# One split load, one moved load, half a value part ahead of five transposes and one dummy pair fewer, in the prologue of a mixed attention and FFN kernel

## Chip, core and metric

The kernel runs on one core of a Trainium2 chip (trn2). The metric is device time in microseconds (us): the median of several executions of the whole kernel. Lower is better. Engines are named as in the profile: PE (matrix engine; PEld is its weight load), DVE (vector), ACT (scalar activations), POOL, and SP, which only issues DMAs. ACT issues some DMAs too; its issues and SP's go into two different DMA queues.

## What is computed

For 2048 tokens of width 640 the result is `g * a + (1 - g) * b`, with a gate per token, a linear attention with 32 heads of width 20, and a SwiGLU FFN of width 1728:

```python
g = sigmoid((x * gate_w).sum(-1, keepdims=True))
# a: q, k, v = split(x @ wqkv); per head
pq, pk = q @ w_phi, k @ w_phi
phi = lambda p: concat(softmax(p), softmax(-p))
kv, z = phi(pk).T @ v, phi(pk).sum(tokens)
a = (phi(pq) @ kv / (phi(pq) @ z + 1e-6)) @ wo
# b
b = (silu(x @ w_gate) * (x @ w_up)) @ w_down
```

Everything is bf16 in memory.

## The kernel before

The 2048 tokens are 16 tiles of 128 (t = 0 to 15); the width of 640 is 5 chunks of 128 (c = 0 to 4). PE contracts over a chunk at a time, so x must stand transposed in `xT[:, t, c, :]`, and a product with 640 output columns is two groups of 320 columns in the two banks of a PSUM pair. There are four such pairs; `next_pair` gives the least recently used one that is not held.

The order of work is written out by hand in two strings. `LOADS` (line 33) gives the order in which the loads are issued; `ORDER` (line 38) gives the order in which every other piece is put into the engines' streams. Each token of the strings is a letter for a helper and its arguments. A tracker (`run`, line 145) adds the semaphore waits that the data needs. So each engine runs its own instructions strictly in the order of the strings, and waits where data or a buffer is not ready.

The pieces that matter here all lie in the first eight microseconds:

- `H` (`warm`, line 511): one dummy pair, that is two 128x128 matmuls on a constant tile. Their result is not used. There are 13 pairs at the head of `ORDER`.
- `X` (`xpose`, line 495): the transposes of token tile t = 0 to 3 by PE, five of them (line 338), and the copies from PSUM into `xT`. For t < 3 the first chunk goes into one bank and is copied by DVE, and the other four go into the second bank. For t = 0 (`X0.0`, `X0.1`) these four are copied by ACT, for t = 1 and 2 by DVE. The token tiles from t = 4 on are transposed by DMAs.
- `G` (`gcol`, line 505): one matmul of 5 columns and a DVE copy which puts the gate's weights beside the value weights, as column 640 of `wvg`.
- `U t.c` (`vpart`, line 539): a value part, the two matmuls (320 and 321 columns; the 321st is the gate's) of token tile t and chunk c of the value projection. Part c = 0 takes a pair and holds it; part c = 4 gives it back and lets ACT copy the result. The parts of the token tiles 0 to 2 are interleaved so that each chunk of weights is used three times soon after it has landed.
- `h` (`load_phi`, line 417) issues two small loads on ACT's queue, after ACT has waited for the landing of the value rows of chunk 3 (`wv_evs[3]`).

The first loads, in the order of `LOADS`, are spread over two queues by the lists `XQ` and `WQ` (lines 391 and 392). SP issues x0 (token tile 0, 160 KB), the gate's weights `gwr`, then the value rows `w1`, `w2`, `w3` (each 128 rows of `A_wqkv` with 640 columns, 160 KB), then the first columns of `wg` and `wu` (`f0`, 480 KB each), and then transposing DMAs (the key weights into `wT`, x4 and so on into `xT`). ACT issues `w0`, x1, x2, x3 and `w4`, and after them loads its function table.

Of the kernel before, what the change touches and what calls it, by code (L numbers as in the profile page):

```python
# [6 lines left out]
P = 128  # L7
S_TOK = 2048
D = 640
# [26 lines left out]
"""  # L36

ORDER = """
H0 H1 H2 H3 H4 H5 H6 H7 H8 H9 H10 H11 H12 X0.0 X0.1 G X1 h U0.0 U1.0 U0.1 X2 U1.1 U2.0 U0.2 U1.2
U2.1 X3 U2.2 U0.3 U1.3 U2.3 U0.4 U1.4 U2.4 V3 Y i4 F0.1 M0 M1 F0.2 M2 V4 M3 M4 F0.0 M5 K0 i3 K1 S0 I  # L40
P0 K3 S1 P1 F1.0 K2 V6 E0 V8 K4 S2 S3 E1 S4 K5 S5 P2 P3 V7 E2 V5 R0 K6 P4 P5 R2 E3 K7 S6 E4 V15 K8
E5 V10 S7 P6 K9 E6 R1 P7 S8 K10 S9 E7 K11 S10 V9 V11 P8 E8 K12 P9 R3 E9 P10 K13 S11 E10 K14 S12 P11
# [11 lines left out]
class _Tracker:  # L54
# [90 lines left out]
    def run(self, eng, fn, reads=(), writes=(), dma=False):  # L145
        rkeys = list(dict.fromkeys(k for a in reads for k in self.keys_of(a)))
        wkeys = list(dict.fromkeys(k for a in writes for k in self.keys_of(a)))
        need = {}

        def req(ev, raw):  # L150
            if ev is None:
                return
            s, v = ev
            if s == eng and not dma and (eng == "pe" or not raw):
                return
            if v > need.get(s, 0):
                need[s] = v

        for k in rkeys:
            for kk in self._conflicts(k):  # L160
                req(self.lastw[kk], True)
                if k[0] == "psum":
                    for s, v in self.readers[kk].items():
                        req((s, v), False)
        for k in wkeys:
            for kk in self._conflicts(k):
                req(self.lastw[kk], True)
                for s, v in self.readers[kk].items():
                    req((s, v), False)
        self._wait(eng, need)  # L170
        ins = fn()
        if dma:
            sn = "d%d" % self.ndma
            self.ndma += 1
            self._add_sem(sn)
            inc = 16
        else:
            sn, inc = eng, 1
        ins.then_inc(self.sem[sn], inc)
        self.cnt[sn] += inc  # L180
        v = self.cnt[sn]
        snap = dict(self.known[eng])
        if not dma:
            snap[sn] = max(snap.get(sn, 0), v)
        self.evknow.setdefault(sn, {})[v] = snap
        ev = (sn, v)
        for k in wkeys:
            self.lastw[k] = ev
            self.readers[k] = {}
        for k in rkeys:  # L190
            r = self.readers[k]
            if r.get(sn, 0) < v:
                r[sn] = v
        return ev


def _build(nc, A_x, A_wqkv, A_w_phi, A_wo, B_x, B_w_gate, B_w_up, B_w_down, gate_w, out):
    tr = _Tracker(nc)
    pe, act, dve, pool, sp = nc.tensor, nc.scalar, nc.vector, nc.gpsimd, nc.sync
# [3 lines left out]
    def sb(name, shape, dtype):  # L203
        t = nc.alloc_sbuf_tensor(name, list(shape), dtype)
        tr.reg(t, "sbuf", nc.lookup_mloc(t).addr)
        return t
# [3 lines left out]
    wvg = sb("wvg", [P, 5, D + 8], BF16)  # L210
# [95 lines left out]
    def bank(b, c0, c1, r0=0, r1=P):  # L306
        return ps[r0:r1, b * 512 + c0:b * 512 + c1]
# [9 lines left out]
    def mm(pairs):  # L317
        reads, writes = [], []
        for p in pairs:
            reads += [p[1], p[2]]  # L320
            writes.append(p[0])

        def fn():
            last = None
            for o, l, r, st, sp_, sk in pairs:
                last = pe.matmul(o, lhsT=l, rhs=r, start=st, stop=sp_, skip_group_check=sk)  # L326
            return last
        return run("pe", fn, list({id(a): a for a in reads}.values()), writes)
# [45 lines left out]
    def dma(e, dst, src, transpose=False):  # L374
        eo = tr.eng[e]

        def fn():
            if transpose:
                return eo.dma_start_transpose(dst, src)
            return eo.dma_start(dst, src)  # L380
        rd = [src] if src.tensor.name in tr.base else []
        wr = [dst] if dst.tensor.name in tr.base else []
        return run(e, fn, rd, wr, dma=True)
# [5 lines left out]


    XQ = ["sp", "act", "act", "act"]
    WQ = ["act", "sp", "sp", "sp", "act"]
    x2 = A_x[0]
    out2 = out[0]

    def load_rows(e, dst, c, c0):
        return dma(e, dst, A_wqkv[c * P:(c + 1) * P, c0:c0 + D])
# [11 lines left out]
    wv_evs = []  # L409

    def load_wv(c):
        wv_evs.append(load_rows(WQ[c], wvg[:, c, 0:D], c, 2 * D))

    def load_gate():
        dma("sp", gwr[0:5, :], bass.AP(gate_w.tensor, gate_w.offset, [[P, 5], [1, P]]))
# [68 lines left out]
    def used(r):  # L484
        ring["lru"].remove(r)
        ring["lru"].append(r)
        return r

    def next_pair():
        return used([r for r in ring["lru"] if r < ring["n"] and r not in held][0])  # L490
# [31 lines left out]
    def v_pairs(t, pr):  # L522
        return [(bank(2 * pr + hb, 0, 320 + hb), xT[:, t, c, :], wvg[:, c, 320 * hb:640 + hb - 320 * (1 - hb)],
                 c == 0, c == 4, False) for c in range(5) for hb in range(2)]

    def v_out(t, pr):
        i = halves(pr).rearrange("p b (h d) -> p b h d", d=DH)
        o = vbuf(t)[:, 0:H * (DH + 1)].rearrange("p (b h d) -> p b h d", b=2, d=DH + 1)[:, :, :, 0:DH]
        copy("act", o, i)
        copy("act", svec[:, t:t + 1], bank(2 * pr + 1, 320, 321))  # L530
# [5 lines left out]

    vpr = {}

    def vpart(t, c):

        if c == 0:
            vpr[t] = next_pair()
            held.add(vpr[t])
        mm(v_pairs(t, vpr[t])[2 * c:2 * c + 2])
        if c == 4:
            held.remove(used(vpr[t]))
            v_out(t, vpr[t])
# [398 lines left out]
    def kv_end():  # L946
# [4 lines left out]

    ops = {
        "H": lambda i: warm(), "i": fills, "X": xpose, "G": gcol, "U": vpart, "V": vtile,
        "M": lambda m: premult(1, m), "R": lambda m: premult(0, m),
        "K": ktile, "S": knorm, "P": kmul, "p": lambda t: kmul(t, "dve"), "E": kvtile, "x": load_x, "t": load_xt, "w": load_wv, "g": load_gate, "h": load_phi, "k": lambda m: load_wt(1, m), "q": lambda m: load_wt(0, m),
        "f": lambda i: load_ffn(FCUT[i], FCUT[i + 1]), "L": load_late_weights, "T": tail_weights, "J": gates,
        "Y": w_blocks, "I": kv_begin, "N": kv_end, "Z": z_row,
# [9 lines left out]
def bass_gated_mix__linear_kernel_hedgehog__swiglu_ffn__prompt_kernel(  # L967
    nc: bass.Bass,
    A_x: bass.AP,
    A_wqkv: bass.AP,  # L970
    A_w_phi: bass.AP,
    A_wo: bass.AP,
    B_x: bass.AP,
    B_w_gate: bass.AP,
    B_w_up: bass.AP,
    B_w_down: bass.AP,
    gate_w: bass.AP,
    out: bass.AP,
):
    _build(nc, A_x, A_wqkv, A_w_phi, A_wo, B_x, B_w_gate, B_w_up, B_w_down, gate_w, out)  # L980
# [28 lines left out]
```

## Time and profile before

| | |
|---|---|
| median of 3 runs | 285.66 us (285.46 to 285.72) |
| the profiled execution | 285.23 us, of which its span from the first to the last instruction is 284.0 us |
| PE busy | 280.9 us, 99% of the span |
| DVE, POOL, ACT busy | 190.5, 156.0, 139.6 us |
| DMA, first 12 us | 2.96 MB, 246 GB/s in the mean |

How to read it: the profile is one execution. A line of the timeline gives the start and the length in us, the engine (a `q` behind its name means its sequencer, here the issue of a DMA), the line of the kernel, the operation, the tiles as out<-in, the shape and how many instructions were merged; in brackets stands how long the engine was idle before it and what ended the idle time. The length of a merged PE line runs to the end of the last matmul, which includes its way through the array, so successive PE lines overlap. The chain of waits goes back from the last instruction to what released it, step by step. The landing of a DMA is the moment at which its semaphore is complete; the trace records each semaphore update.

### The profile page before, as it was taken

Reading aid. Unit: us, or ns where it says so; the run is one execution under the profiler, and the core shown is the slowest. Engines: PE = TensorE matmul, PEld = TensorE weight load, DVE = VectorE, ACT = ScalarE, POOL = GpSimd, SP = SyncE. Lnnn points to the kernel's source line nnn. Section 1 sums busy time; section 2 is a strip of 40 time slices with the busy share of each in tenths; the row PEclk is TensorE's granted clock in tenths of the full one; section 3 lists DMA queues with packets and bytes.
Section 4 is the critical chain, followed back from the end, with each engine's and each line's share of the span. In section 5 each row is a group of like instructions: output and inputs, shape, how many; then the busy total and the mean of one; then the engine's idle time right before and its main releaser. Section 6 shows DMA issues by size and latency. Waiting matters only on the chain.

```text
span 284.0 us, 4689 instructions
## 1 busy us (share of the span) xinstructions
PE 280.9 (99%) x1802; PEld 156.3 (55%) x1809; DVE 190.5 (67%) x280; ACT 139.6 (49%) x241; POOL 156.0 (55%) x119
## 2 busy tenths in 40 slices
PE   8999999999999999999999999999999999999997
PEld 7656777766645455445545445454544444444766
DVE  2336767684798888879999899997878355053100
ACT  2567777785755666657747764130101675001022
POOL 6277979987178858597868744463062553100100
PEclk9999999999999999999999999999999999999999
DMA  7976879100085252022340200623647510133411
GB/s 236 231 115 118 122 169 374 36 3 0 3 264 155 64 107 51 9 54 51 60 52 2 52 4 14 134 57 66 122 133 139 101 37 7 42 80 71 122 46 46
DMA packets 62085, 25.19 MB, mean 89 GB/s; under 512 B 51023, under 2 KB 61543, under 8 KB 62063
## 3 DMA queue, kind: packets, MB, share of 16 engines
q1 hardware_dynamic: 60534, 24.03, 37.4%
q10 hardware_dynamic: 1529, 0.87, 1.0%
q8 instruction: 14, 0.23, 0.4%
q14 instruction: 8, 0.07, 0.1%
HBM read 10.16 MB, written 2.63 MB: 45 GB/s over the span
## 4 chain that ended last, share of the span: by engine, by line
PE 99%; issue 0%; DVE 0%
PE ps L326 97%; PE ps L518 1%; PE ps L338 1%; DVE osb L934 0%
## 5 line engine op out<-in xcount | busy, mean ns | idle before, releaser
L354 POOL TENSOR_TENSOR hT<-hT,us 128x512 bf16<-128x512 bf16 (+1 forms) x37 | 43.6, 1185 | 43.4 <-DVE hT L358 33.6
L326 PE MATMUL ps<-xT,wg 128*128 128x512 bf16 x260 | 64.6, 379 | 0.0
L326 PE MATMUL ps<-xT,wu 128*128 128x512 bf16 x260 | 64.6, 379 | 0.0
L354 POOL TENSOR_TENSOR ph<-eq,qc 128x1320 bf16<-128x1320 bf16 x16 | 40.3, 2521 | 30.6 <-DVE qc L673 19.5
L326 PE MATMUL ps<-wqk,xT 128*128 128x320 bf16 x320 | 47.9, 299 | 0.0
L344 ACT ACTIVATE us<-ps 128x512 bf16<-128x512 f32 (+1 forms) x56 | 33.4, 597 | 22.0 <-PE ps L326 19.7
L326 PEld LDWEIGHTS ps<-xT,wu 128*128 128x128 bf16 x260 | 25.4, 98 | 30.7
L326 PEld LDWEIGHTS ps<-xT,wg 128*128 128x128 bf16 x260 | 24.9, 98 | 28.4 <-ACT oT L344 0.6
L354 POOL TENSOR_TENSOR ekr<-ekr,krec 128x1280 bf16<-128x1280 bf16 x16 | 37.3, 2357 | 5.8 <-DVE krec L368 5.8
L358 DVE SCALAR_TENSOR_TENSOR hT<-hT,ps 128x512 bf16<-128x512 bf16 (+1 forms) x37 | 25.0, 681 | 21.2 <-ACT hT L344 19.0
L344 ACT ACTIVATE eq<-ps 128x640 bf16<-128x640 f32 x32 | 22.3, 703 | 32.3 <-PE ps L326 31.2
L326 PEld LDWEIGHTS ps<-wqk,xT 128*128 128x128 bf16 x320 | 30.4, 98 | 13.3
L354 POOL TENSOR_TENSOR hx<-hx,us 128x512 bf16<-128x512 bf16 (+1 forms) x19 | 24.1, 1271 | 21.3 <-DVE hx L358 11.8
L344 ACT ACTIVATE hT<-ps 128x512 bf16<-128x512 f32 (+1 forms) x37 | 22.0, 596 | 25.0 <-PE ps L326 24.8
L365 DVE TENSOR_REDUCE ksum<-ekr 128x64 f32<-128x1280 bf16 x16 | 23.4, 1463 | 11.0 <-ACT ekr L344 11.0
L326 PE MATMUL ps<-hT,wd 128*128 128x512 bf16 (+1 forms) x137 | 30.6, 380 | 0.2
L344 ACT ACTIVATE ekr<-ps 128x640 bf16<-128x640 f32 x32 | 22.3, 703 | 6.9 <-PE ps L326 6.4
L326 PE MATMUL ps<-wvg,xT 128*128 128x320 bf16 (+1 forms) x160 | 24.1, 300 | 0.0
L365 DVE TENSOR_REDUCE qw<-ez 128x64 f32<-128x1280 bf16 x16 | 23.6, 1476 | 0.0
L365 DVE TENSOR_REDUCE qz<-eq 128x64 f32<-128x1280 bf16 x16 | 23.6, 1477 | 0.0
L354 DVE TENSOR_TENSOR ez<-eq,zb 128x1280 bf16<-128x1280 bf16 x16 | 21.9, 1385 | 0.3 <-DMA zb<-zrow 0.3
L326 PEld LDWEIGHTS ps<-hT,wd 128*128 128x128 bf16 (+1 forms) x140 | 13.0, 97 | 16.2 <-issue 1.3
(103 smaller groups left out, 288.5 us busy)
## 6 DMA issues: line engine op xcount, KB each, us to landing
wd<-in_B_w_down_dram SPq DMA_DIRECT2D x1, 2080.0 KB, 10.6
out_dram<-osb SPq DMA_DIRECT2D x2, 640.0 KB, 3.5
wg<-in_B_w_gate_dram SPq DMA_DIRECT2D x1, 1040.0 KB, 8.8
wu<-in_B_w_up_dram SPq DMA_DIRECT2D x1, 1040.0 KB, 9.9
wog<-in_A_wo_dram SPq DMA_DIRECT2D x2, 375.0 KB, 4.4
wg<-in_B_w_gate_dram SPq DMA_DIRECT2D x1, 640.0 KB, 5.2
wu<-in_B_w_up_dram SPq DMA_DIRECT2D x1, 640.0 KB, 6.4
omgb<-omgd SPq DMA_DIRECT2D x2, 256.0 KB, 4.0
```

Of the source, the lines that this page charges most:

```text
L326: last = pe.matmul(o, lhsT=l, rhs=r, start=st, stop=sp_, skip_group_check=sk)
L338: last = pe.transpose(o, i, ident[0:k, 0:k])
L344: return run("act", lambda: act.activation(o, i, func, scale=scale), rd, [o])
L354: return run(e, lambda: eo.tensor_tensor(o, a, b, op), [a, b], [o])
L358: return run("dve", lambda: dve.scalar_tensor_tensor(out=o, in0=a, scalar=s, in1=b, op0=op0, op1=op1), rd, [o])
L365: return run("dve", lambda: dve.tensor_reduce(o, i, AX.X, ALU.add), [i], [o])
L518: last = pe.matmul(bank(2 * pr, 0, P), lhsT=c, rhs=c, start=True, stop=True)
```

## The change

Four edits:

1. The value rows of chunk 0 are loaded by two DMAs of 320 columns (80 KB each) in place of one of 640 (160 KB), both on ACT's queue and still at its head. x1, x2 and x3 are issued behind both.
2. The value rows of chunk 4 are issued by SP, behind those of chunk 3 and ahead of `wg`, in place of ACT behind x3.
3. The value part U0.0 is cut into its two matmuls: `U0.0.0` (columns 0 to 319) stands behind `G` and ahead of x1's transposes, and `U0.0.1` (columns 320 to 640) stands where U0.0 stood. The first takes the pair.
4. There are 12 dummy pairs in place of 13.

The number of DMAs that ACT issues ahead of its function table stays five; SP issues one more. On PE's stream the only differences are two dummy matmuls fewer and one matmul of 320 columns five transposes earlier. The order of instructions on DVE, POOL and ACT (apart from its DMA issues) is the same.

```diff
 ORDER = """
-H0 H1 H2 H3 H4 H5 H6 H7 H8 H9 H10 H11 H12 X0.0 X0.1 G X1 h U0.0 U1.0 U0.1 X2 U1.1 U2.0 U0.2 U1.2
+H0 H1 H2 H3 H4 H5 H6 H7 H8 H9 H10 H11 X0.0 X0.1 G U0.0.0 X1 h U0.0.1 U1.0 U0.1 X2 U1.1 U2.0 U0.2 U1.2
...
     XQ = ["sp", "act", "act", "act"]
-    WQ = ["act", "sp", "sp", "sp", "act"]
+    WQ = ["act", "sp", "sp", "sp", "sp"]
...
     def load_wv(c):
-        wv_evs.append(load_rows(WQ[c], wvg[:, c, 0:D], c, 2 * D))
+        if c == 0:
+            dma(WQ[c], wvg[:, c, 0:320], A_wqkv[0:P, 2 * D:2 * D + 320])
+            wv_evs.append(dma(WQ[c], wvg[:, c, 320:D], A_wqkv[0:P, 2 * D + 320:3 * D]))
+        else:
+            wv_evs.append(load_rows(WQ[c], wvg[:, c, 0:D], c, 2 * D))
...
-    def vpart(t, c):
-
-        if c == 0:
+    def vpart(t, c, hb=None):
+
+        if c == 0 and not hb:
             vpr[t] = next_pair()
             held.add(vpr[t])
-        mm(v_pairs(t, vpr[t])[2 * c:2 * c + 2])
+        mm(v_pairs(t, vpr[t])[2 * c + (hb or 0):2 * c + (2 if hb is None else hb + 1)])
```

## The prediction

> **What bounds the kernel now.** I read the page's chain of waits first, then the chain in order of time, then the timeline of the first 30 us, then the trace's semaphore records for the exact landings. The page's chain:
>
> ```profile
> PE 99%; issue 0%; DVE 0%
> PE ps L326 97%; PE ps L518 1%; PE ps L338 1%; DVE osb L934 0%
> ```
>
> PE sets the end, and nothing else holds a share. From the chain in order of time:
>
> ```profile
> 0.84 2.93 PE ps L518 x26
> 3.78 0.02 issue
> 3.79 0.72 PE ps L338 x5
> ...
> 7.91 66.79 PE ps L326 x630
> ```
>
> I went through the starts of all matmuls for places where the next one comes later than the columns of the one before it allow. From 5.29 us on there is none worth naming (a 128-column matmul follows in 56 ns, a 320-column one in 136 ns; the jumps of 0.2 us far behind are matmuls missing from the records). So everything from U1.0's first matmul at 5.29 us on is a stream without a hole, and a change confined to the prologue can do only three things: move 5.29, tear a hole into the stream, or change PE's pace. The prologue:
>
> ```profile
> 0.81 0.41 ACTq L380 DMA_DIRECT2D wvg<-in_A_wqkv_dram  x1
> ...
> 0.84 2.93 PE L518 MATMUL ps<-const-bfloat16-1.0 128*128 128x128 bf16 x26 [0.84 <-PEq L994]
> ...
> 1.26 1.42 ACTq L380 DMA_DIRECT2D xs<-in_A_x_dram  x3
> ...
> 3.19 1.28 ACT L344 ACT_TABLE_LOAD   x1 [3.19 <-issue]
> ...
> 3.79 0.45 PEld L338 LDWEIGHTS ps<-ident,xs 128*128 128x128 bf16 x5 [0.28 <-DMA xs<-in_A_x_dram]
> ...
> 4.12 0.23 DVE L350 COPY xT<-ps 128x128 bf16<-128x128 bf16 x1 [4.12 <-PE ps L338]
> ...
> 4.41 0.70 PE L338 MATMUL ps<-ident,xs 128*128 128x128 bf16 x5
> 4.55 0.60 ACT L344 ACTIVATE xT<-ps 128x512 bf16<-128x512 bf16 x1
> ...
> 4.91 1.08 PE L326 MATMUL ps<-wvg,xT 128*128 128x320 bf16 x6
> ...
> 5.26 0.40 PEld L326 LDWEIGHTS ps<-wvg,xT 128*128 128x128 bf16 x4 [0.21 <-issue]
> ...
> 5.83 0.44 PE L338 MATMUL ps<-ident,xs 128*128 128x128 bf16 x5
> ```
>
> The reader is to see three things. (a) x0's transposes start at 3.79 on x0's landing (3.75 in the semaphore records), not on the end of the dummies: the weight load sat idle 0.28 us for the DMA. The last dummy starts at 3.465 and the dummies follow each other in 0.107 us, so PE ran dry at 3.57. (b) The gap of 0.21 us before 5.26 stands as "issue", but the instruction waits for ACT's copy of x0's other four chunks (4.55 to 5.15), both because U0.1 reads them and because U1.0's PSUM pair is the one that this copy empties. That copy began behind x0's last transpose (done at 4.52) and behind ACT's table load, which ended at 3.19 + 1.28 = 4.47. (c) PE runs at half pace at first: five transposes take 0.70 at 4.41 and 0.44 at 5.83; the starts are 0.107 us apart, then 0.056. The trace's first record of the full granted clock begins at 4.96.
>
> **One dummy pair fewer.** It removes 2 x 0.107 = 0.21 us of PE time in front of x0's transposes. PE would be dry at 3.36 in place of 3.57, and x0 lands at 3.75. Worth nothing: a wait of 0.22 becomes one of 0.43. It would be worth up to 0.21 only if x0 landed by 3.36.
>
> **The half part ahead of x1's transposes.** x0's first chunk is copied by DVE at 4.12 to 4.35, its semaphore comes at 4.36, and a matmul that waits for such a copy starts some 0.06 later (U2.0: semaphore 6.32, matmul 6.38). So U0.0.0 starts at about 4.42, just where x1's first transpose stood (4.41), and 320 columns at the half pace cost 2.5 x 0.107 = 0.27: x1's transposes start at 4.68. Three of them at 0.107 and two at 0.056 end at 5.11; U0.0.1 takes 0.14, and PE is at U1.0 by 5.25. Two waits hold U1.0 there. ACT's copy is unchanged, so its matmul is not before 5.29. And U1.0 reads x1's first chunk: from the first transpose of x1 to the semaphore of its copy were 4.97 - 4.41 = 0.56 us, so it now comes at 4.68 + 0.56 = 5.24, and U1.0 starts at about 5.31. **Sum: 5.31 - 5.29 = +0.02 us.** PE does the same work between 3.79 and 5.3 in another order, between the same two ends. Cover: x1's landing, which was 4.36, with PE asking for it at 4.40, may now come as late as 4.64. Behind U1.0 nothing is nearer: x1's second copy would end at about 5.8, and U1.1 reads it at 6.11.
>
> The most that can be won: if x0 landed earlier, ACT's copy still could not begin before 4.47 plus the 0.08 or less that it stood behind it. So 5.29 can go to about 5.21, and **-0.08 us is the floor** of the prologue as the change leaves it. PE can win no more by being early.
>
> **The split load.** ACT issues five DMAs ahead of its table before and after (0.81, three from 1.26 in 1.42, one at 2.70), so the table load stays at 3.19. x1, x2 and x3 are issued one step, about 0.48 us, later: 1.74, 2.22, 2.70. Their packets did not start at their issue but 2.0 to 2.5 us later (x1 issued 1.26, first packet 3.26; x2 1.74, 3.87; x3 2.22, 4.74), each within 0.05 us of the end of the block before it on the queue. The DMA engines are full from about 3 us on. So the later issue is hidden by the backlog, and what counts is what the split costs there. Rows of 640 bytes are not in the trace; the packet records give 36 ns for 768 bytes and 55 ns for 1280, so about 31 for 640 on the same line. A block of 160 KB is 8 rows on each of 16 engines: 8 x (2 x 31 - 55) = 0.06 us. From the other side, if a DMA of 128 rows costs a slot whatever its bytes, the split delays all that is behind it by one slot: the blocks start 0.4 to 0.5 us apart, say 0.45. Below nothing: x0 shares the engines with shorter packets, and may land up to 0.1 earlier, worth at most the 0.08 above. I take +0.06, as the row nearest in size gives it. The landings against PE's need (weight load) before:
>
> | | x1 | w1 | x2 | w2 | x3 | w3 | w4 |
> |---|---|---|---|---|---|---|---|
> | landed | 4.36 | 4.77 | 5.51 | 6.49 | 6.90 | 7.37 | 7.67 |
> | asked for | 4.40 | 5.42 | 5.70 | 6.53 | 7.34 | 7.89 | 8.70 |
>
> The thinnest margin is w2's, 0.04 us (one engine's update came 0.45 behind the other fifteen). With +0.06 PE waits 0.02 less the 0.02 by which it is itself late: nothing. With +0.45 it waits 0.4.
>
> [...]
>
> **The fifth rows on SP.** The bytes are the same and the engines are full until about 10 us, so the last of `wg` and `wu` lands as before (9.00 and 10.49; PE asks at 10.9 and 11.9). w4 itself now stands right behind w3 (7.37) and a block takes 0.45 us: 7.8 at the latest, or 8.3 with a slot's delay of w3, and 8.70 is asked. SP's issues behind it move by one issue, 0.43 us: `wg`, `wu`, and all transposes. The first of these is issued at 4.05 and takes 2.94 to issue, so it stood in a backlog that absorbs this. If it did not, the first key weights (landed 11.06, asked 12.96) have 1.9 us and the second (12.71, asked 13.39) 0.7. ACT's small loads wait for w3 (issue at 7.39 behind 7.37); w3 is no longer in competition with w4 and comes rather earlier. Their product is ready at 12.71 and PE loads it at 12.96: 0.25 us of cover. Cost: nothing.
>
> **The sum.** +0.02 (order) + 0 (dummies) + 0 (loads) on the profiled execution: 285.25. The profiled one is 0.43 below the median of 285.66; on the median that makes **285.7 us**, which is no change.
>
> **Rivals.**
>
> *PE's holes are closed.* PE is dry 0.22 us before 3.79 and 0.07 before 5.29. If in ordinary runs x0 lands earlier than here, or the shorter rows let it, both are won: -0.29, 285.4. For it: the profile is one execution, 0.43 from the median. Against it: ACT's table load, which holds U1.0 at 5.21 or later.
>
> *A DMA costs a slot.* The split puts 0.45 us on x1, x2, w2 and x3. PE waits at x1 (4.81 for 4.68), and in the end for w2, some 0.4 us in all, since each wait gives cover to the next: 286.1. For it: the issue takes 0.41 to 0.46 us whatever it moves, and the blocks' starts fit a slot as well as they fit the bytes. Against: the DMA share of 1.05 from 3 us on, which is full engines.
>
> *PE's clock comes later* (slower). The full clock came 4.1 us after the first dummy, with PE busy but for 0.22 us. With 0.43 us dry before x0's transposes the count could begin anew at 3.79, and the full clock come at 7.9 in place of 4.96. PE would run its stream from 4.96 to 7.9 at half pace and lose half of 2.9 us: +1.5, 287.2. It decides between an idle time of 0.22 us, which is shown to do no harm, and one of 0.43. For it: nothing in the rows but the removed pair. Against: the half part puts 0.27 us of matmul back before 4.96.
>
> [...]
>
> **Chances.** Forecast 0.62, holes closed 0.15, a slot 0.13, the clock 0.07, what I do not see 0.03. About 0.2%, 0.57 us, is what a measurement of this kernel can tell from no change: below 285.1 or above 286.2. The forecast, the holes and nearly all of the slot lie inside. Faster 0.04, slower 0.14 (the clock 0.07, a slot with a second wait 0.05, the rest), within 0.82. The range runs from the holes' 285.4 less the 0.2 by which the runs shown fall below their median, 285.2, to the slot's 286.1, and leaves out the clock.
>
> **What would show it.** Right: x0's transposes still start at x0's landing near 3.8 with an idle time of 0.4 before them; x1's transposes at 4.7; U1.0 at 5.3; x2's transposes at 5.8; no PE wait behind. Wrong: U1.0 before 5.2 or after 5.5; PE weight loads idle on `xs` or `wvg` between 5 and 8 us (a slot); x2's transposes 0.1 us apart (the clock).

## The result, and the profile after

The changed kernel takes 288.64 us (median of 4 runs, 288.12 to 288.90), the kernel before 285.56 us beside it. The ratio is 1.0088, 95% interval 1.006 to 1.0116: slower by 3.1 us (0.9%), clear of the noise, where 285.2 to 286.1 us were predicted. The profiled execution took 288.90 us with a span of 287.6; the one before took 285.23 with 284.0.

The page's chain of waits, after:

```profile
PE 97%; DMA 2%; ACTq 0%; DVE 0%; issue 0%
PE ps L326 96%; DMA xs<-in_A_x_dram 2%; ACTq L380 0%; PE ps L338 0%; DVE osb L938 0%
```

Before, PE alone stood there. Now a DMA into `xs`, one of x1 to x3, holds 2% of the span, and ACT's issue queue is in the chain. The chain in order of time (start, length, what) says where:

```profile
1.73 0.46 ACTq L380
2.18 0.03 issue
2.21 5.53 DMA xs<-in_A_x_dram
7.74 0.05 issue
7.78 0.45 PE ps L338 x5
8.24 2.64 PE ps L326 x10
10.88 0.53 PE ps L338 x5
11.41 66.92 PE ps L326 x630
```

It goes back from x2's transposes at 7.78 to x2's load, issued at 2.21, and to ACT's issues. From 11.41 on PE is again a stream of 66.92 us (66.79 before) and stays one to the end. So the loss lies ahead of 11.4 us. The timeline there, with the idle time of each engine in brackets:

```profile
3.18 1.28 ACT L344 ACT_TABLE_LOAD   x1 [3.18 <-issue]
...
3.49 0.45 PEld L338 LDWEIGHTS ps<-ident,xs 128*128 128x128 bf16 x5 [0.20 <-DMA xs<-in_A_x_dram]
3.50 0.71 PE L338 MATMUL ps<-ident,xs 128*128 128x128 bf16 x5
...
4.10 0.45 PE L326 MATMUL ps<-wvg,xT 128*128 128x320 bf16 x1
...
4.47 0.60 ACT L344 ACTIVATE xT<-ps 128x512 bf16<-128x512 bf16 x1
...
6.45 0.28 PEld L338 LDWEIGHTS ps<-ident,xs 128*128 128x128 bf16 x5 [2.25 <-DMA xs<-in_A_x_dram]
6.46 0.45 PE L338 MATMUL ps<-ident,xs 128*128 128x128 bf16 x5 [1.91 <-DMA xs<-in_A_x_dram]
...
6.75 0.98 PE L326 MATMUL ps<-wvg,xT 128*128 128x321 bf16 x5
...
7.78 0.28 PEld L338 LDWEIGHTS ps<-ident,xs 128*128 128x128 bf16 x5 [0.39 <-DMA xs<-in_A_x_dram]
7.78 0.45 PE L338 MATMUL ps<-ident,xs 128*128 128x128 bf16 x5
...
8.07 2.80 PE L326 MATMUL ps<-wvg,xT 128*128 128x320 bf16 x10
...
10.67 0.74 PE L338 MATMUL ps<-ident,xs 128*128 128x128 bf16 x5
...
11.21 3.61 PE L326 MATMUL ps<-wvg,xT 128*128 128x320 bf16 x24
```

Three things are to be seen. First, x0 came earlier than before: its transposes start at 3.50, not at 3.79, and the half part is done on time, at 4.10. Second, PE then stands still until 6.46, for x1, which landed at 6.41 by the semaphore records (4.36 before), and again at 7.78 for x2. x2's transposes stand 7.78 - 5.83 = 1.95 us later than before. Third, ten value matmuls take 2.80 us from 8.07 and five transposes 0.74 at 10.67, where the five at 7.78 took 0.45: PE is back at half pace. Busy time and granted clock of the four stretches of 3.41 us around this (columns: stretch, its length, busy time and number of instructions for each engine, granted clock, DMA share, GB/s):

```profile
core 0: us, PE busy (x) PEld busy (x) DVE busy (x) ACT busy (x) POOL busy (x), PEclk, DMA share, GB/s
1.32:4.73 3.41, 3.23 (x29) 2.63 (x26) 0.41 (x2) 1.54 (x2) 3.10 (x9) 1.00 0.69 185
4.73:8.14 3.41, 1.63 (x16) 1.01 (x17) 0.74 (x3) 0.34 (x1) 0.96 (x3) 1.00 1.00 310
8.14:11.55 3.41, 3.41 (x19) 2.10 (x17) 0.66 (x3) 0.00 (x0) 0.00 (x0) 0.50 1.22 265
11.55:14.97 3.42, 3.42 (x26) 2.41 (x25) 1.44 (x4) 2.02 (x7) 1.73 (x4) 1.00 1.12 177
```

The clock's column is full by default where the trace has no record, as for the first stretch, where the dummies stand 0.107 us apart, as x3's transposes do in the stretch recorded at 0.50 (x2's at 7.78: 0.056). The records are: full at 4.73 for 3.413 us, half from 8.143 for 3.413, full from 11.556 on. In the stretch from 4.73 to 8.14 PE was busy 1.63 of 3.41 us, and in the one behind it the clock was 0.50. PE never ran dry there, so half of 3.41, 1.71 us, was lost. Waits and clock together are 1.95 + 1.71 = 3.66 us; the two profiled executions are 288.90 - 285.23 = 3.67 us apart. So the two terms account for the whole difference between them.

What is left to explain is why x1 was 2 us late. DMA rates between 3.2 and 5.0 us, before and after (same columns):

```profile
3.20:5.00 1.80, 1.78 (x18) 1.46 (x16) 0.60 (x3) 1.73 (x2) 1.74 (x4) 1.00 1.03 341
```

```profile
3.20:5.00 1.80, 1.35 (x11) 0.76 (x8) 0.41 (x2) 1.79 (x2) 1.74 (x4) 1.00 0.85 206
```

341 GB/s before, 206 after (the last number). The engines moved fewer bytes just when x1 was waited for, while their busy share fell only from 1.03 to 0.85, so single packets took longer. So it was not the number of bytes ahead of x1 that held it up.

### The profile page after: what moved, and what is told of

Its sections match the earlier page's. It is cut to its first block, busy times and chain, and to the rows that moved or that the text cites. A ratio compares the mean times of both kernels' runs of the same rounds, so it can differ in the third digit from the quotient of the medians.

```text
span 287.6 us, 4695 instructions
## 1 busy us (share of the span) xinstructions
PE 282.9 (98%) x1807; PEld 156.9 (55%) x1807; DVE 193.0 (67%) x280; ACT 139.6 (49%) x241; POOL 155.4 (54%) x119
## 4 chain that ended last, share of the span: by engine, by line
PE 97%; DMA 2%; ACTq 0%; DVE 0%; issue 0%
PE ps L326 96%; DMA xs<-in_A_x_dram 2%; ACTq L380 0%; PE ps L338 0%; DVE osb L938 0%
## 5 line engine op out<-in xcount | busy, mean ns | idle before, releaser
L354 POOL TENSOR_TENSOR hT<-hT,us 128x512 bf16<-128x512 bf16 (+1 forms) x37 | 42.9, 1167 | 45.5 <-DVE hT L358 33.2
L326 PE MATMUL ps<-wvg,xT 128*128 128x320 bf16 (+1 forms) x160 | 25.9, 312 | 0.0
L354 DVE TENSOR_TENSOR ez<-eq,zb 128x1280 bf16<-128x1280 bf16 x16 | 22.6, 1430 | 1.2 <-DMA zb<-zrow 1.2
```

The lines of the kernel that those rows point to most:

```text
L354: return run(e, lambda: eo.tensor_tensor(o, a, b, op), [a, b], [o])
```

## The experiments

The first four take the edits apart.

**e1_split_only**, edit 1 alone on the kernel before:

```diff
     def load_wv(c):
-        wv_evs.append(load_rows(WQ[c], wvg[:, c, 0:D], c, 2 * D))
+        if c == 0:
+            dma(WQ[c], wvg[:, c, 0:320], A_wqkv[0:P, 2 * D:2 * D + 320])
+            wv_evs.append(dma(WQ[c], wvg[:, c, 320:D], A_wqkv[0:P, 2 * D + 320:3 * D]))
+        else:
+            wv_evs.append(load_rows(WQ[c], wvg[:, c, 0:D], c, 2 * D))
```

> The kernel before with edit 1 alone: w0 in two column halves, w4 still issued by ACT (its sixth load), U0.0 whole and behind x1's transposes, 13 dummy pairs. Split theory (the halves' 256 short rows at the head of ACT's queue hold up what is behind them): x1 lands near 6.4 instead of 4.4, DMA share under 0.6 between 3.2 and 4.5 us, 288 to 289 us. Move theory (the fifth value rows on SP's queue take descriptors and engine time from ACT's): x1 lands within 0.1 of 4.4, 285.4 to 285.8 us. Order theory (two dummies fewer and the half part let the clock fall): 285.4 to 285.8 us.

Measured: 288.52 us, ratio 1.008 (1.0052 to 1.0107), x1 at 6.72, 188 GB/s between 3.2 and 5. The DMA share from 3.2 to 4.5 was 0.90, not under 0.6 as expected: the engines were busy, but moved little. Within the spread the split alone is the whole loss, with all 13 dummy pairs in place.

**e2_w4_on_sp**, edit 2 alone:

```diff
-    WQ = ["act", "sp", "sp", "sp", "act"]
+    WQ = ["act", "sp", "sp", "sp", "sp"]
```

> The kernel before with edit 2 alone: w4 issued by SP behind w3. Split theory: x1 lands near 4.4 and nothing moves, 285.4 to 285.8 us. Move theory: x1 lands 1 to 2 us late, 287 to 289 us. Order theory: no change.

Measured: ratio 0.9988 (0.9974 to 1.0002), x1 at 4.36: no change, and the move theory falls. Not foreseen was x2 in the profile: it landed at 6.39 (5.51 before), and PE waited 0.47 us for it.

**e3_order_only**, edits 3 and 4 alone (`ORDER` and `vpart` of the changed kernel, the loads of before).

> The changed kernel's stream for PE with the loads of before: U0.0.0 ahead of x1's transposes and 12 dummy pairs (edits 3 and 4). Split and move theory: x1 lands near 4.4, its transposes start at 4.68 as predicted, U1.0 near 5.3, 285.4 to 285.8 us. Order theory: the full clock comes 3.4 us later or falls again, 287 us or more.

Measured: ratio 1.001 (0.9991 to 1.003), x1 at 4.42. Its timeline:

```profile
4.48 0.32 PE L326 MATMUL ps<-wvg,xT 128*128 128x320 bf16 x1
...
4.63 0.44 PE L338 MATMUL ps<-ident,xs 128*128 128x128 bf16 x5
...
5.36 0.70 PE L326 MATMUL ps<-wvg,xT 128*128 128x320 bf16 x4 [0.15 <-ACT xT L344]
...
5.94 0.45 PE L338 MATMUL ps<-ident,xs 128*128 128x128 bf16 x5
```

The half part starts at 4.48, x1's transposes at 4.63 (predicted 4.68), U1.0 at 5.36 with x0 landing 0.07 later than in the profile before, x2's at 5.94. The order theory falls: 0.3 us without work ahead of x0's transposes (they sat idle until 3.87 here) did not hold the clock back.

**e4_unsplit**, the changed kernel with w0 in one load, and **e12_unsplit5**, the same program in more rounds:

```diff
-        if c == 0:
-            dma(WQ[c], wvg[:, c, 0:320], A_wqkv[0:P, 2 * D:2 * D + 320])
-            wv_evs.append(dma(WQ[c], wvg[:, c, 320:D], A_wqkv[0:P, 2 * D + 320:3 * D]))
-        else:
-            wv_evs.append(load_rows(WQ[c], wvg[:, c, 0:D], c, 2 * D))
+        wv_evs.append(load_rows(WQ[c], wvg[:, c, 0:D], c, 2 * D))
```

> The changed kernel with w0 in one load again (edits 2, 3 and 4). x1 is then again ACT's second issue. Split theory: x1 near 4.4, 285.4 to 285.8 us. Move theory: x1 late, 287 to 289 us. Order theory: 287 us or more with x1 on time.

> The same program as e4_unsplit (the changed kernel with w0 in one load), in more rounds, as the version that may beat both. If its lead is real, the ratio to the kernel before is 0.997 to 0.9995 with an interval that ends below 1; if it was the spread of the runs, the interval takes in 1.

Measured: 0.9979 (0.9961 to 0.9997) the first time, with x1 at 4.33, and 1.0 (0.9982 to 1.0019) the second. The lead of the first was the spread of the runs. No version here beats the kernel before.

The next ones ask what it is about the split: its short rows, the further load, or that x1 is issued later.

**e6_gap**, w0 in one load whose rows are cut in two by a gap in the destination (`w0h` lies in memory that is free at that time), on the kernel before:

```diff
+        if c == 0:
+            wv_evs.append(dma(WQ[c], w0h[:, :, 0:320],
+                              A_wqkv[0:P, 2 * D:3 * D].rearrange("p (b k) -> p b k", b=2)))
```

> The kernel before with w0 in one load whose rows are cut in two by a gap in its destination: 128 x 2 runs of 640 bytes, one issue, x1 issued at 1.26 as before (one small DVE copy is added for the gate's column). Short-row theory: x1 lands 1 us or more late and the time is 287 us or more. Theory of the extra load, and of the later issue: x1 near 4.4, 285.4 to 286.2 us.

Measured: 1.001 (0.9983 to 1.0036), x1 at 4.51, 256 packets of 640 bytes in the records, 32 ns each. Short rows cost nothing (31 ns were estimated). That theory falls.

**e7_late**, w0 whole, and a load of 5 rows into an unused tile between w0 and x1 on ACT's queue:

```diff
         wv_evs.append(load_rows(WQ[c], wvg[:, c, 0:D], c, 2 * D))
+        if c == 0:
+            late.append(dma("act", spare[0:5, :], bass.AP(gate_w.tensor, gate_w.offset, [[P, 5], [1, P]])))
```

> The kernel before with a load of 5 rows of 256 bytes into an unused tile between w0 and x1 on ACT's queue, so that x1, x2, x3 and w4 are issued one step later and w0 stays whole. Theory of the later issue: x1 near 6.5, 288 to 289 us. Short-row theory: x1 within 0.2 of 4.4, 285.4 to 286.3 us. Theory of the extra load: in between, since the load is an extra one but of 5 rows alone; near 286 us if its rows count.

Measured: 287.72 us, ratio 1.0068 (1.0048 to 1.0087), x1 at 5.79. 1.2 KB ahead of x1 cost it 1.4 us. The landing lies between the 6.5 of the later issue and the theory of the extra load, which allowed a time near 286; the time is nearer to the former. The DMA rates:

```profile
3.20:5.00 1.80, 1.29 (x12) 0.86 (x9) 0.41 (x2) 1.30 (x2) 1.74 (x4) 1.00 0.97 243
```

**e5_rows** and **e11_rows_free**, w0 in two loads of 64 whole rows. In e5 the tracker held the second load back until the first had landed, so ACT issued it at 3.40 and x1 at 3.99: 294.34 us, ratio 1.0307 (1.028 to 1.0334), x1 at 11.49. That run shows what a wait in ACT's queue costs, not what the split costs. e11 has no such wait:

```diff
+            dma(WQ[c], wvg[0:64, c, 0:D], A_wqkv[0:64, 2 * D:3 * D])
+            wv_evs.append(run(WQ[c], lambda: act.dma_start(wvg[64:P, c, 0:D], A_wqkv[64:P, 2 * D:3 * D]), dma=True))
```

> The kernel before with w0 in two loads of 64 whole rows (1280 bytes each, 80 KB each) in place of two column halves; all else as before. Short-row theory (256 rows of 640 bytes do it): x1 lands within 0.2 of 4.4 us, 285.4 to 286.3 us (ACT's table load comes one issue later). Theory of the extra load (a second load at the head of ACT's queue does it, whatever its rows): x1 near 6.5, 288 to 289 us. Theory of the later issue (x1 issued at 1.73 for 1.26): the same, 288 to 289 us.

> The kernel before with w0 in two loads of 64 whole rows, issued one behind the other without the wait that e5_rows had between them (PE's first value part waits for both). x1 is ACT's third issue. Place theory, and the theory of the added load: x1 lands at 5.5 to 6.7 us, 287 to 289 us. Short-row theory: x1 near 4.4, 285.4 to 286.3 us.

Measured, e11: 288.27 us, ratio 1.0067 (1.0031 to 1.0102), x1 at 6.60. Rows of full length in the same two loads do the same harm.

**e9_swap** adds no load at all. It exchanges x1 and x2 on ACT's queue, on the kernel before:

```diff
-x0 w0 x1 g w1 x2 w2 x3 w3 w4 f0 ...
+x0 w0 x2 g w1 x1 w2 x3 w3 w4 f0 ...
```

> The kernel before with x1 and x2 exchanged on ACT's queue (w0, x2, x1, x3, w4): no load is added and none is cut, x1 is ACT's third issue (1.74) in place of its second. Place theory (ACT's third load lands between 5.5 and 6.7 us whatever it is, as x2 did in the kernel before and in the kernels with w0 whole): x1 lands at 5.5 to 6.7, x2 near 4.4, PE waits 1.1 to 2.2 us before x1's transposes, 286.8 to 289 us. Theory of the added load (the transfers are held up only because there is one more of them early): x1 lands at 4.8 at the latest, one block of 0.45 behind, PE waits 0.4 us, 285.9 to 286.5 us.

Measured: 288.14 us, ratio 1.0068 (1.0042 to 1.0095), x2 at 4.31 and x1 at 5.22. The landing falls between the two theories (5.5 to 6.7, and 4.8 at the latest); the time is that of the place theory, though with a shorter wait. PE waits 0.81 us for x1:

```profile
5.27 0.45 PEld L338 LDWEIGHTS ps<-ident,xs 128*128 128x128 bf16 x5 [0.98 <-DMA xs<-in_A_x_dram]
5.27 0.71 PE L338 MATMUL ps<-ident,xs 128*128 128x128 bf16 x5 [0.81 <-DMA xs<-in_A_x_dram]
...
7.38 0.74 PE L338 MATMUL ps<-ident,xs 128*128 128x128 bf16 x5
...
7.92 2.36 PE L326 MATMUL ps<-wvg,xT 128*128 128x320 bf16 x10
...
10.11 0.44 PE L338 MATMUL ps<-ident,xs 128*128 128x128 bf16 x5
```

A wait of 0.81 us became a loss of 2.4 in the median: the transposes at 7.38 still run 0.107 us apart, those at 10.11 at full pace. The clock, which is full by about 5 in the profile before, came only near 9.7 here (read from the pace; this profile has no clock record). Its runs lie from 286.17 to 288.81 us, the lowest three 0.4 to 0.8 above the kernel before; that would fit the wait alone, but those runs have no profile. The DMA engines were full meanwhile:

```profile
3.20:5.00 1.80, 1.26 (x12) 0.86 (x9) 0.40 (x2) 1.78 (x2) 1.74 (x4) 1.00 1.04 346
```

**e10_half_sp**, the changed kernel with the second half of w0 on SP's queue, ahead of w1, so that x1 is ACT's second load again:

```diff
-x0 w0 x1 g w1 x2 w2 x3 w3 w4 f0 ...
+x0 w0 x1 g b w1 x2 w2 x3 w3 w4 f0 ...
...
+    def load_half():
+        dma("sp", wvg[:, 0, 320:D], A_wqkv[0:P, 2 * D + 320:3 * D])
```

> The changed kernel with the second half of w0 on SP's queue, behind the gate's weights and ahead of w1: the split and the short rows stay, x1 is again ACT's second issue, and w1 to w4 are each one place later on SP's queue. Place theory: x1 lands within 0.2 of 4.4 and PE starts x1's transposes at 4.7 or earlier; what is late now is w1 (4.8 before), at 5.3 to 6.7 us, and PE waits for it at most 1.2 us: 285.6 to 287.2 us. Theory of the added load: x1 is late as well, near 6 us, 287.5 to 289 us.

Measured: 287.28 us, ratio 1.0052 (1.0027 to 1.0076). x1 landed at 3.91, earlier than expected, and its transposes started at 4.29, earlier than in any other kernel. The lateness moved to the other queue: the half, SP's third load, landed at 5.84 and w1, the fourth, at 6.73, just beyond what was expected, as is the time.

**e8_fill** asks about the clock: 15 more dummy pairs in the wait for x1.

```diff
-... X0.0 X0.1 G U0.0.0 X1 h U0.0.1 ...
+... X0.0 X0.1 G U0.0.0 H20 H21 ... H34 X1 h U0.0.1 ...
```

> The changed kernel with 15 more dummy pairs between the half part and x1's transposes, which fill PE's wait for x1. If the loss of 3.1 us is 1.4 to 2 us of waiting and the rest the clock's fall in the window after the wait, x1 still lands near 6.4 and the time is 287 to 287.4 us with the full clock from 4.7 us on. If it is all waiting, the time stays at 288.3 to 289 us.

Measured: 287.44 us, ratio 1.0064 (1.0047 to 1.0082), the full clock from 6.80 us on without a break.

```profile
4.05 0.45 PE L326 MATMUL ps<-wvg,xT 128*128 128x320 bf16 x1
...
4.29 3.06 PE L522 MATMUL ps<-const-bfloat16-1.0 128*128 128x128 bf16 x30
...
7.19 0.44 PE L338 MATMUL ps<-ident,xs 128*128 128x128 bf16 x5
...
8.28 0.44 PE L338 MATMUL ps<-ident,xs 128*128 128x128 bf16 x5
```

The fill was too long: x1 had landed at 5.87, but the dummies ran at half pace nearly throughout and held PE until 7.19. Its stream is later than the changed kernel's (x2's transposes at 8.28 for 7.78) and the median is still 1.2 us lower; the clock did not fall. That fits the two terms, though the time is just above the 287.4 that was expected and the expected moment of the clock (4.7) was wrong.

That a late x1 and a fall of the clock are two things is shown more directly by the profiles of e7 and of e13 (below). There x1 landed at 5.79 and 6.50, but the transposes behind the wait ran at full pace, 0.056 us apart, and the spans are 1.9 and 2.0 us above the one before, not 3.7.

Last, three kernels about what holds up the third load, each with one run; x1's landing is what counts in them.

**e13_f0_late** issues `wg` and `wu` behind three transposes, **e14_sp_hold** lets SP wait for x3's landing before it issues anything behind w4, **e15_w1_hold** lets it wait for x1's landing before w1 (all on the changed kernel; `v` is a wait of SP for an x load):

```diff
-... w3 w4 f0 k0 k1 t4 k2 ...
+... w3 w4 k0 k1 t4 f0 k2 ...        (e13)
+... w3 w4 v3 f0 k0 k1 t4 k2 ...     (e14)
+x0 w0 x1 g v1 w1 x2 ...             (e15)
```

> The changed kernel with the first columns of wg and wu (640 rows each) issued by SP behind three transposing loads in place of ahead of them. PE waits for them later, so the time itself says little; the landing of x1 is what counts. If the long loads issued from 3.5 us on hold up x1, x1 lands at 4.8 or earlier; if not, at 5.2 to 6.7 as before.

> The changed kernel with SP waiting for x3's landing before it issues anything behind w4 (wg, wu, the transposes): nothing but the nine first loads is in the queues until then. If any later load or transpose holds up x1, it lands at 4.8 or earlier and x2 at 5.3 or earlier; if the first loads hold up each other, x1 lands at 5.2 to 6.7 and the DMA share stays under 0.9 between 3.2 and 5 us.

> The changed kernel with SP waiting for x1's landing before it issues w1: up to then only x0, the two halves, the gate's weights and ACT's x1, x2, x3 are in the queues. If w1 to w4 on the other queue hold up x1, it lands at 4.5 or earlier. If the third load on ACT's queue is late by itself, it lands at 5.2 to 6.7 with the engines half empty.

Measured (287.24, 286.79 and 289.94 us): x1 at 6.50, 5.71 and 4.98. What SP issues behind w4 is not the cause: e8, with the same loads as the changed kernel, had x1 at 5.87 (6.41 in the changed kernel), so single landings differ by half a microsecond anyway. SP's loads beside x1 seem to have a share in it: without them it landed at 4.98, earlier than expected of a load that is late by itself (5.2 to 6.7) and later than if they were all of it (4.5). With nothing in SP's queue but x0 and the gate's weights x1 still landed 0.6 us later than as second load before, with the engines at 242 GB/s:

```profile
3.20:5.00 1.80, 1.27 (x11) 0.76 (x8) 0.40 (x2) 1.79 (x2) 1.74 (x4) 1.00 0.83 242
```

By the packet records x1's rows came slowly at first, 9, 22 and 32 in the three quarters of a microsecond from 3.25 on, with single packets of up to 0.7 us; then the queue moved 58 to 72 rows a quarter.

**What the runs show together.** Landings of ACT's first three loads, from the semaphore records:

| kernel | first | second | third | x1's place |
|---|---|---|---|---|
| before | w0 3.94 | x1 4.36 | x2 5.51 | 2 |
| e2 | w0 3.95 | x1 4.36 | x2 6.39 | 2 |
| e3 | w0 4.02 | x1 4.42 | x2 5.89 | 2 |
| e4 | w0 3.99 | x1 4.33 | x2 6.05 | 2 |
| e6 | w0 4.08 | x1 4.51 | x2 5.46 | 2 |
| e10 | half 3.58 | x1 3.91 | x2 6.03 | 2 |
| e9 | w0 3.91 | x2 4.31 | x1 5.22 | 3 |
| e7 | w0 3.93 | 5 rows 4.24 | x1 5.79 | 3 |
| e11 | 64 rows 3.54 | 64 rows 5.57 | x1 6.60 | 3 |
| e1 | half 3.61 | half 3.88 | x1 6.72 | 3 |
| after | half 3.61 | half 3.79 | x1 6.41 | 3 |

The third load on ACT's queue lands between 5.2 and 6.7 in all of these, whatever it carries and however little stands ahead of it (4.98 in e15, where w1 was held back). PE asks for x2 at 5.70 and loses little by that (0.47 us in e2's profile); it asks for x1 at 4.4 and loses much. The split put x1 into the third place. That this is what made x1 late is shown by e9, which does it with no split and no further load, and by e10, which keeps the split and takes x1 out of that place.

What it is about the third place is not shown. The third load on ACT's queue is also issued later (x1 at 1.73 to 2.05 in place of 1.26) and, but for e15, behind SP's w1 (1.66), which before came after x1; no run delays x1 without putting a load ahead of it, so place and moment of issue are not told apart. Nor is a third place late on every queue: w1 is SP's third load, behind x0 and the 5 rows of the gate's weights, and landed at 4.4 to 5.0 in the kernels with w0 whole, but at 5.2 to 6.5 in those with two halves ahead of x1 on the other queue. And in e11 the second load was late already (5.57).

Why a place costs this much stays open in part. With full engines (e9) it is 5.22 - 4.36 = 0.86 us, about two blocks of 0.43; w1 of the other queue landed in between, at 5.03. With less ahead of it than in e9 (after, e1, e7) it is 1.4 to 2.4 us, and the engines fall to 188 to 243 GB/s. There it is the rows that are slow, not the start: in the changed kernel x1's first row started at 3.52, only 0.26 us later than before, but its 128 rows (in the order of the queue) lasted until 5.74 in place of 3.90, at 89 ns in the mean in place of 55, the longest 0.95 us. Later loads are excluded as the main cause by e13 and e14. What makes the third load's packets come slowly even with nearly nothing beside them (e15) is in no record of the trace.

Whether the late load costs the clock too differs. By the pace of the matmuls (128 columns in 0.107 us at the half clock, in 0.056 at the full one) PE had a stretch at the half clock behind its wait in the profiles of after, e1, e9, e11 and e15, and none in those of e7, e10, e13 and e14. What decides between them no run isolates.

## Why the prediction was wrong

- *What bounds the kernel.* Right: from the prologue's end on PE is a stream without a hole, and all of the 3.67 us lies ahead of 11.6 us.
- *One dummy pair fewer, and the half part.* Right: e3 makes both edits with the loads of before, with a ratio of 1.001 (0.9991 to 1.003). That x1's transposes stood at 4.63 for a predicted 4.68 is in part luck: the half part started 0.06 us later than predicted, but took 0.15 in place of 0.27, since the full clock was there at 4.53 and not at 4.96.
- *The fifth rows on SP.* Right in the time, 0.9988 in e2. The landings were not as predicted: w4 came at 8.29 in e2, for 7.8 at the latest, and x2 at 6.05 to 6.39 in the three profiles with this edit and w0 whole (e2, e4, e12), for 5.46 to 5.89 in those without it and x1 on time (before, e3, e6). Whether the edit does that is not shown.
- *The split load.* Here it failed, at "the later issue is hidden by the backlog, and what counts is what the split costs there". The split's own cost was right (32 ns a packet, e6), but it isn't what counts. x1 lost its place in the queue and landed at 6.41 in place of 4.36, where 0.06 us were priced and 0.28 us of cover (4.64) were there. Part of the price stood in the prediction's own table: x2, then ACT's third load, landed at 5.51, 1.15 us behind x1, and x1 was about to take that place. I read the cover from the queue's packet starts (each block begins where the one before it ends) and took each block to last as long as before. The start was indeed nearly hidden (0.26 us later); the block's length was not the same: x1's rows took 2.2 us in place of 0.64. Nor were the DMA engines "full from about 3 us on" after the change: they ran at 206 GB/s from 3.2 to 5.
- *The rival "a DMA costs a slot"* named the mechanism and x1 and w2 as the places, with a chance of 0.13. Its slot was mis-sized: 0.45 us, the distance between blocks of alternating queues. With w1 in between it is two such blocks (0.86 in e9), and x1 came 2.05 us later in the changed kernel (6.41 - 4.36).
- *The rival "PE's clock comes later"* had nearly the right price (1.5 us; 1.71 measured) and the wrong trigger. It is not the idle time ahead of x0's transposes, which was 0.2 us after and harmless, but the wait for x1. And the two rivals are not alternatives: behind a late load the full clock can fall or come late too (it fell here and came late in e1, e9 and e11; neither shows in the profiles of e7 and e13). Here both came, 1.95 + 1.71 us; they were priced one or the other, and the range left out the clock.

## What to carry to other kernels

Price a load by its place in its queue, not by its bytes alone (x1 landed at 4.36 as ACT's second load, and at 5.79 as its third behind 1.2 KB more, in e7): look up when the load that stands there now lands, and ask whether the engine can wait that long for the one that is to stand there. That landing is a first price, not a sure one: 5.51 stood in the table, 6.41 came, and in the table of landings above x1 as third load stands at 5.22 (e9) to 6.72 (e1). A further load ahead, even one of 1.2 KB, can cost as much as a large one: 1.4 us in e7, 0.86 in e9 with the 160 KB of x2. Near the first full clock, price a wait both without and with a half-pace stretch behind it: both occurred here (a span 1.9 us longer in e7, 3.7 in the changed kernel).

## What was not expected of the hardware

- A load of 5 rows of 256 bytes cost the load behind it on the same queue 1.4 us (e7).
- ACT's third load started slowly even with nothing more in SP's queue (9, 22 and 32 rows in the three quarters of a microsecond from 3.25 on), and the same queue alone then moved 344 GB/s from 4 to 5 us (e15).
- In the changed kernel's profile PE busy for 3.23 of 3.41 us was followed by the full clock; busy for 1.63 of 3.41, by the half clock for the whole of the next 3.41 us. With a wait of 0.81 us ahead of the first full clock that came only at about 9.7 us (e9); yet with a wait of 1.32 us the transposes behind it were at full pace (e7).
- The full clock began at 4.5 to 6.8 us by five records (among them 4.53 in e3, 4.73 in the changed kernel, 4.96 before, 6.80 in e8; 13.31 in e15, behind two waits), with the first dummy always at 0.84, and in e4 x0's transposes ran at full pace from 3.8 on. Part of the spread of the runs may come from that; no run here isolates it.
